# One core, a Fourier mixing block: a difference kept in PSUM, batch 0's inverse as one whole float32 product, and a self-paired channel by its sum less twice one part

## The chip, the cores and the metric

The kernel runs on one core of one Trainium2 chip. The metric is the time of one execution in device microseconds. Times are written in us, stretches of the run as us from the start of the profiled span. L905 is line 905 of the kernel before.

## The reference

The input x has 8 batches of 3136 tokens with 256 channels. Each batch is filtered along the tokens in the frequency domain, the result is mixed by a two-dimensional Fourier transform whose real part is added to it, and each token then goes through a normalisation and a two-layer perceptron with a residual:

```python
def _attn_ref(x, filt_r, filt_i):
    Y = np.fft.rfft(x, axis=1) * (filt_r + 1j * filt_i)[None]
    return np.fft.irfft(Y, n=x.shape[1], axis=1).astype(np.float32)

def _moe_ref(x, w_ch1, w_ch2):              # x is what _attn_ref gave
    mixed = np.real(np.fft.fft(np.fft.fft(x, axis=1), axis=2)).astype(np.float32)
    u = x + mixed
    un = (u - mean(u)) / sqrt(var(u) + 1e-6)
    return u + np.maximum(un @ w_ch1, 0.0) @ w_ch2      # 256 -> 1024 -> 256
```

The token transform of the filtered signal is the spectrum Y itself, so the kernel mixes straight from Y and needs the inverse transform only for the residual u.

## The kernel before

**Work and tiles.** Per batch: `first` and `spectrum` are the two stages of the forward transform (112 x 28 points), `spectrum` with the filter behind it. `inverse1` and `inverse2` are the two stages of the inverse (7 chunks `ch` or `c` each), with a turn through DRAM between them (`d2`, written from tile `bt`, read back as `b2`). `fold` makes sums and differences of channel pairs for the channel transform (`ef`, then `eo` as a float16 high and low part), `bring` scales the inverse and sends it to DRAM (`dy`). The tokens are then taken in 49 groups `g` of 256 pairs of rows: `fetch` loads the group's residual (`pages<-dy`, L1030), `prepare` adds the channel mixing (L1071 products, L1096 and L1121 additions) and makes the norm's statistics, `normalize` gives `ut`, and `products` runs eight steps per group: six products into `h` (L1318), `rectify` (ACT L1346, DVE L1348) and twelve products into `acc` (L1359), added to the residual in L1373. Batches 1 to 7 split each float32 operand into a float16 high and low part and run three float16 passes; batch 0 is worked in float32 where the time before the first step is concerned.

**Order.** Everything is placed by `Plan`, a planner in the program: each task yields its next engine with an estimated duration, takes buffers from rings of fixed size (`take`, `give`), and the planner writes down one fixed order per engine. On the chip each engine runs its list strictly in that order. The four PSUM banks of ring `psf` serve `first`, `spectrum` (from batch 1), both inverse stages and the mixing; the products have banks of their own (`psh`, `pso`). Ring `x16` holds three 2 KB scratch buffers, ring `ast` three buffers for DRAM writes. Almost all DMAs are issued from SP's one queue.

**The places that are touched.** In `inverse1` PE gives two banks per chunk, `ps[0]` and `ps[1]`, each from 64 x 64 corners of the array (L873, with L863 for the first chunk). From batch 1, ACT copies `ps[1]` to SBUF (L891), DVE makes sum and difference into SBUF (L895), ACT casts both to float16 (L901) and the low parts are the float32 value less the cast, both read from SBUF:

```python
            for i in range(2):
                pool_ = i >= LOW_ON_DVE[b > 1]
                yield ("POOL", 1.16) if pool_ else ("DVE", 0.65)
                (nc.gpsimd if pool_ else nc.vector).tensor_tensor(
                    bt[:, :, 1, i], sums[i], bt[:, :, 0, i], op=ALU.subtract
                )
```

(L905: batch 1 both on DVE, later batches one on DVE and one on POOL.) For batch 0 `inverse1` copies the two banks out as they are (L914) and sum and difference are made after the turn, in `inverse2`, by two DVE instructions per chunk on SBUF (L953). The float32 table `i1f` of batch 0 is later turned in place into the float16 table `i1` by `split_back` (ACT L679 and L681, POOL L683). `fold` sets row 0 of the difference, the channel pair that is its own mirror, by one more subtraction on one partition (L822 on DVE for batch 0, L825 on POOL after).

Of the kernel before, what the change touches and what calls it, by code (L numbers as in the profile page):

```python
# [37 lines left out]
TWIN = 0.83  # L38
BACKED = 6.5
LOW_ON_DVE = (2, 1)  # L40
# [168 lines left out]
def constants():  # L209
# [30 lines left out]
    even[0] = p % 2 == 0  # L240
# [44 lines left out]
    def both_halves(a):  # L285
# [5 lines left out]
    i1f = both_halves(i1.reshape(112, 29, 64).astype(np.float32))  # L291
# [11 lines left out]
        "c_i1f": np.ascontiguousarray(i1f),  # L303
        "c_i2f": both_halves(i2f),
# [11 lines left out]
def _program(ctx, tc, nc, a, NB):  # L316
# [46 lines left out]
    i1 = cp.tile([120, 29, 2, 64], F16, name="i1")  # L363
# [11 lines left out]
    i1f = i1.rearrange("p j l u -> p (j l u)").bitcast(F32).rearrange("p (j u) -> p j u", u=64)  # L375
# [10 lines left out]
    def z_page(ch):  # L386
        return pages[:, (ch + YBUFS) % (YBUFS + 2)].rearrange("p (l j c) -> p l j c", l=1, c=256)
# [41 lines left out]
    y16s = [cp.tile([128, 2, 8, 64], F16, name=f"y16_{h}") for h in range(4)]  # L429
    for t in y16s:  # L430
        nc.gpsimd.memset(t[:, :, :, 56:], 0.0)
# [131 lines left out]
    def first(b, q, t):  # L563
# [39 lines left out]
        home = (*("ast",) * 3, "un", "un", "u16", "u16", *("h",) * 4)[q % 11] if b == 0 else "ast"  # L603
        k = yield take(home)
        pool, bufs = (fp, 3) if home == "ast" else (mp, 4 if home == "h" else 2)
# [44 lines left out]
    def load_tables():  # L650
# [6 lines left out]
        for ch in range(7):  # L657
            yield "SP" if ch == 0 else "calm", 0.5, -78
            j = slice(4 * ch + (ch > 0), 4 * ch + 5)
            nc.sync.dma_start(i1f[:, j], a["c_i1f"][:, j])  # L660
# [11 lines left out]
    def split_back():  # L672
        yield until(("backs",))
        for ch in range(7):
            j = slice(4 * ch + (ch > 0), 4 * ch + 5)
            k = yield take("x16")
            whole = fp.tile([120, 4 + (ch == 0), 64], F32, tag="x16", name=f"i1f_{ch}", bufs=3)
# [6 lines left out]
            give("x16", k)  # L684
            done("i1", ch)

    def by_part(b, yt):
# [3 lines left out]
        v = yt.rearrange("p h (j s q) -> p h j s q", j=4, s=2)[..., :56]  # L691
        return v.rearrange("p h j s (r q) -> p h r j s q", r=2)

    def spectrum(b, ch, hf, t):
# [4 lines left out]
        if hf == 0:  # L699
# [3 lines left out]
            n = 448 if b else 512  # L703
            yts[b, ch] = k, pool.tile([128, 2, n], F32, tag=home, name=f"yt_{b}_{ch}", bufs=2), home
            if b == 0:
                yield "POOL", 0.2
                nc.gpsimd.memset(yts[b, ch][1].rearrange("p h (j q) -> p (h j) q", q=64)[:, :, 56:], 0.0)
# [56 lines left out]
        if b == 0:  # L764
            kp = yield take("psh")
            pt = spare(f"yT_{ch}_{hf}").rearrange("p (j c) -> p j c", j=4)
            yield "PE", 0.7
            for j in range(4):
                nc.tensor.transpose(pt[:, j], yt[:, hf, 128 * j : 128 * j + 128], ident)
# [3 lines left out]
            nc.scalar.copy(zs[b, ch][:, 0, :, 128 * hf : 128 * hf + 128], pt)  # L773
            give("psh", kp)
            done("z", b, ch, hf)
            return
        k = yield take(f"y16_{hf}")
# [18 lines left out]
    def fold(b, ch, t):  # L796
# [12 lines left out]
        if ch == 0:  # L809
# [4 lines left out]
            nc.vector.tensor_copy(es[:1, 1:2], ef[:1, 1, 0, 0:1])  # L814
# [783 lines left out]
```

## Time and profile before

| | |
|---|---|
| runs | 1465.88, 1466.61, 1467.34; median 1466.61 |
| profiled execution | 1467.97, its span 1466.2 |
| first step's product starts | 124.68 |
| busy share of the span | PE 92%, DVE 74%, ACT 58%, POOL 49% |
| mean granted TensorE clock | 0.963 |

The span is the time from the first to the last instruction of the profiled execution, which itself took 1.4 us more than the median run. PE's busy time counts pipelined matmuls, so two engines' shares are not alike. The granted clock is 1 at 2.4 GHz and 0.5 at 1.2 GHz.

### The profile page before, as it was taken

Reading aid. Unit: us, or ns where it says so; the run is one execution under the profiler, and the core shown is the slowest. Engines: PE = TensorE matmul, PEld = TensorE weight load, DVE = VectorE, ACT = ScalarE, POOL = GpSimd, SP = SyncE. Lnnn points to the kernel's source line nnn. Section 1 sums busy time; section 2 is a strip of 40 time slices with the busy share of each in tenths; the row PEclk is TensorE's granted clock in tenths of the full one; section 3 lists DMA queues with packets and bytes.
Section 4 is the critical chain, followed back from the end, with each engine's and each line's share of the span. In section 5 each row is a group of like instructions: output and inputs, shape, how many; then the busy total and the mean of one; then the engine's idle time right before and its main releaser. Section 6 shows DMA issues by size and latency. Waiting matters only on the chain.

```text
span 1466.2 us, 33150 instructions
## 1 busy us (share of the span) xinstructions
PE 1356.0 (92%) x12693; PEld 906.8 (62%) x12693; DVE 1082.1 (74%) x2199; ACT 850.3 (58%) x1605; POOL 719.9 (49%) x893
## 2 busy tenths in 40 slices
PE   4647998869999999999999999999999998999998
PEld 1423565547666666666666766667666665666666
DVE  5797688776778698787878787778858788564543
ACT  4367456754567557764577567755566664444341
POOL 2631197126861488325961776338833398132220
PEclk8757999989999999999999999999999999999999
DMA  8966788759696889769887989669794997643330
GB/s 279 261 187 191 193 161 202 195 174 227 138 230 191 192 192 200 189 176 241 172 221 217 203 199 230 178 166 218 170 252 128 226 193 158 158 114 107 93 85 29
DMA packets 359933, 268.89 MB, mean 183 GB/s; under 512 B 217751, under 2 KB 295007, under 8 KB 359775
## 3 DMA queue, kind: packets, MB, share of 16 engines
q1 hardware_dynamic: 359775, 266.79, 74.5%
q8 instruction: 99, 1.62, 0.5%
q14 instruction: 59, 0.48, 0.1%
HBM read 113.10 MB, written 102.76 MB: 147 GB/s over the span
## 4 chain that ended last, share of the span: by engine, by line
PE 61%; DVE 13%; POOL 7%; DMA 6%; issue 6%; ACT 5%; SPq 1%; DVEq 0%; POOLq 0%; ACTq 0%
PE h L1318 25%; PE acc L1359 24%; PE s L601 3%; PE y L968 2%; DMA x<-x 2%; DMA d<-ast 2%; DVE bt L905 2%; PE mix L1071 2%; PE i L873 2%; DVE h L1348 1%; DVE pages L1096 1%; DMA at<-d 1%; DVE t L743 1%; POOL y L784 1%; DVE st L1236 1%
## 5 line engine op out<-in xcount | busy, mean ns | idle before, releaser
L1359 PE MATMUL acc<-w2s,h 128*128 128x256 f16 x4704 | 589.7, 273 | 11.9 <-DVE pages L1373 11.9
L1318 PE MATMUL h<-ut,w1s 128*128 128x512 f16 x2352 | 580.4, 383 | 14.6 <-DVE h L1348 8.8
L1359 PEld LDWEIGHTS <-h 128*128 128x128 f16 x4704 | 453.1, 98 | 146.2 <-issue 25.7
L1348 DVE SCALAR_TENSOR_TENSOR h<-h,h 128x512 f16<-128x512 f32 x392 | 268.2, 685 | 250.4 <-ACT h L1346 249.2
L1346 ACT ACTIVATE h<-h 128x512 f16<-128x512 f32 x392 | 232.8, 594 | 295.0 <-PE h L1318 286.4
L1318 PEld LDWEIGHTS <-w1s 128*128 128x128 f16 x2352 | 225.8, 98 | 228.2 <-issue 28.4
L1293 POOL TENSOR_TENSOR u<-un,u 128x512 f16<-128x512 f32 x94 | 110.6, 1177 | 274.1 <-ACT u L1287 258.5
L1267 ACT ACTIVATE un<-pages,sb 128x256 f32<-128x256 f32 x196 | 109.6, 593 | 27.2 <-DVE sb L1217 24.4
L1121 POOL TENSOR_TENSOR pages<-sm,pages 128x508 f32<-128x508 f32 x48 | 61.8, 1289 | 122.7 <-ACT sm L1159 100.1
L837 POOL TENSOR_TENSOR eo<-ef,eo 128x448 f16<-128x448 f32 (+6 forms) x62 | 61.5, 996 | 100.6 <-ACT eo L834 70.7
L784 POOL TENSOR_TENSOR y<-yt,y 128x448 f16<-128x448 f32 x98 | 104.4, 1070 | 12.3 <-ACT y L782 12.0
L757 POOL TENSOR_TENSOR yt<-yt,t 128x224 f32<-128x224 f32 x98 | 67.5, 688 | 78.4 <-DVE t L743 77.9
L743 DVE SCALAR_TENSOR_TENSOR t<-s,pF,ft 128x448 f32<-128x448 f32 x126 | 83.7, 671 | 8.9 <-PE s L725 8.9
L1096 DVE SCALAR_TENSOR_TENSOR pages<-mix,alpha,pages 128x254 f32<-128x254 f32 (+2 forms) x188 | 83.5, 476 | 4.9 <-ACT sm L1159 3.5
L1236 DVE BATCH_NORM_STATS2 st<-pages 128x6 f32<-128x256 f32 x196 | 80.3, 410 | 8.9 <-POOL pages L1127 7.2
L993 ACT ACTIVATE ys<-y,alpha 128x512 f32<-128x512 f32 x110 | 70.9, 685 | 25.5 <-PE y L968 25.1
L782 ACT CAST y<-yt 128x448 f16<-128x448 f32 x98 | 54.9, 563 | 49.3 <-POOL yt L759 47.6
L905 DVE TENSOR_TENSOR bt<-sd,bt 128x512 f16<-128x512 f32 x56 | 79.5, 1428 | 0.6 <-ACT bt L901 0.6
L743 DVE SCALAR_TENSOR_TENSOR yt<-s,pF,ft 128x448 f32<-128x448 f32 x98 | 65.9, 673 | 15.6 <-PE s L725 14.8
L601 PE MATMUL s<-x,s 112*112 112x512 f16 x252 | 67.5, 390 | 9.5 <-DVE x L578 5.8
L895 DVE TENSOR_TENSOR sd<-i,sd 128x512 f32<-128x512 f32 x98 | 66.9, 682 | 12.0 <-ACT sd L891 10.2
L905 POOL TENSOR_TENSOR bt<-sd,bt 128x512 f16<-128x512 f32 x42 | 50.3, 1197 | 51.1 <-ACT bt L901 43.2
(171 smaller groups left out, 1800.0 us busy)
## 6 DMA issues: line engine op xcount, KB each, us to landing
x<-x SPq DMA_DIRECT2D x56, 448.0 KB
d<-ast SPq DMA_DIRECT2D x112, 224.0 KB
at<-d SPq DMA_DIRECT2D x56, 448.0 KB
d<-bt SPq DMA_DIRECT2D x112, 224.0 KB
pages<-d SPq DMA_DIRECT2D x112, 224.0 KB
out<-pages SPq DMA_DIRECT2D x98, 256.0 KB
pages<-dy SPq DMA_DIRECT2D x92, 256.0 KB
dy<-ys SPq DMA_DIRECT2D x96, 224.0 KB
```

What stands on the lines that cost most here:

```text
L601: nc.tensor.matmul(p, s1[:, hs], x16[:, hx], start=i == 0, stop=i == 2)
L743: nc.vector.scalar_tensor_tensor(out, p, pF[:, 1:2], f, op0=ALU.mult, op1=ALU.mult)
L784: nc.gpsimd.tensor_tensor(y16v[:, 1], yh, y16v[:, 0], op=ALU.subtract)
L905: (nc.gpsimd if pool_ else nc.vector).tensor_tensor(bt[:, :, 1, i], sums[i], bt[:, :, 0, i], op=ALU.subtract)
L1096: nc.vector.scalar_tensor_tensor(out, p, al, y, op0=ALU.mult, op1=ALU.add)
L1236: nc.vector.bn_stats(st[:, 2 * t + k], y[:, t, k])
L1267: nc.scalar.activation(un[:, k], y[:, t, k], AF.Identity, bias=sb[:, i, 1:2], scale=sb[:, i, 3:4])
L1293: nc.gpsimd.tensor_tensor(u16[:, :, :, 1], unv, u16[:, :, :, 0], op=ALU.subtract)
L1318: nc.tensor.matmul(p.rearrange("p (t k q) -> p t k q", t=2, k=2), w1s[:, d, hw, 128 * f : 128 * f + 128], utv[:, :, :, d, hx], start=i == ...
L1346: nc.scalar.activation(h[:, 0], p, AF.Relu)
L1348: nc.vector.scalar_tensor_tensor(h[:, 1], p, 0.0, h[:, 0], op0=ALU.max, op1=ALU.subtract)
L1359: nc.tensor.matmul(acc[:, kind], h[:, hh, c0 : c0 + 128], w2s[:, f, hw], start=f == 0 and kind == 0 and i == 0, stop=f == 7 and kind == 1 ...
```

## The change

Three things are done, and the buffers are laid out anew for them.

1. `inverse1` from batch 1: the difference is written back into PSUM, over `ps[1]`, and its cast and its low part are read from there. The sum goes into the scratch buffer `total` (batch 1: into PSUM, over `ps[0]`). In later batches cast and low part of the sum are a task of their own, `low_half`, on ACT and POOL. One scratch buffer is taken in place of two; the banks are held for longer.
2. Batch 0: `inverse1_whole` makes sum and difference in the product itself, with a table of 112 x 112 per slot in float32 (four products of 256 columns per chunk, two per bank, on the whole array), and `inverse2` reads them without an addition. Each half chunk is stored by two DMAs of 1 KB rows. Transposes and DRAM rows of batch 0 lose their padding and its memsets. The larger `i1f` shares its memory (`late`) with `i1` and with the `y16` buffers, so `i1` comes by DMA and `y16` is cleared after batch 0's last inverse product (`load_back`).
3. `fold`: row 0 of the difference becomes minus twice the second part (one ACT instruction on one partition), and the mixing table's row 0 is all ones, so that sum and minus twice one part make what was the difference.

The last three DRAM writes of batch 0's `first` go through `x16` buffers instead of waiting for `ast`, and the planner's start for batch 0's `inverse1` is moved from 6.5 to 3.8 steps.

```diff
-TWIN = 0.83
+TWIN = 0.86
+PASSES = ((0, 0), (1, 0), (0, 1))
-LOW_ON_DVE = (2, 1)
...
-    i1 = cp.tile([120, 29, 2, 64], F16, name="i1")
+    late = cp.tile([128, 2048 + 1856], F32, name="late")
+    i1f = late[:112, :3136].rearrange("p (j u) -> p j u", u=112)
+    i1 = late[:120, 2048:].bitcast(F16).rearrange("p (j l u) -> p j l u", l=2, u=64)
...
-        home = (*("ast",) * 3, "un", "un", "u16", "u16", *("h",) * 4)[q % 11] if b == 0 else "ast"
+        home = (*("ast",) * 3, "un", "un", "u16", "u16", *("h",) * 4, *("x16",) * 3)[q] if b == 0 else "ast"
...
-    def split_back():
-        yield until(("backs",))
-        for ch in range(7):
-            yield "ACT", 0.35
-            nc.scalar.copy(whole, i1f[:, j])
-            yield "ACT", 0.35
-            nc.scalar.copy(i1[:, j, 0], whole)
-            yield "POOL", 0.6
-            nc.gpsimd.tensor_tensor(i1[:, j, 1], whole, i1[:, j, 0], op=ALU.subtract)
+    def load_back():
+        yield until(("backs",))
+        yield "POOL", 0.7
+        nc.gpsimd.memset(y16a.rearrange("p i l j q -> p (i l j) q")[:, :, 56:], 0.0)
+        done("y16")
+        for i in range(2):
+            yield "calm", 1.7
+            j = slice(0, 13) if i == 0 else slice(13, 29)
+            nc.sync.dma_start(i1[:, j], a["c_i1"][:, j])
...
 def fold(b, ch, t):
-        if b == 0:
-            yield "DVE", 0.52
-            nc.vector.tensor_tensor(eft[:1, 1], yt[:1, 0, 0], yt[:1, 1, 0], op=ALU.subtract)
-        else:
-            yield "POOL", 0.64
-            nc.gpsimd.tensor_tensor(eft[:1, 1], yt[:1, 0, 0], yt[:1, 1, 0], op=ALU.subtract)
+        yield "ACT", 0.4
+        nc.scalar.activation(eft[:1, 1], yt[:1, 1, 0], AF.Copy, scale=-2.0)
...
+    def inverse1_whole(ch, h, t):
+        yield until(("z", 0, ch, 0), ("z", 0, ch, 1), ("i1f", ch))
+        kp = yield take("psf")
+        j = 4 * ch + 2 * h
+        p = bank(f"i1_0_{ch}_{h}")[:112].rearrange("p (j c) -> p j c", j=2)
+        yield "PE", 1.0
+        for i in range(2):
+            nc.tensor.matmul(p[:, i], i1f[:, j + i], zs[0, ch][:, 2 * h + i], start=True, stop=True)
+        k = yield take("ast")
+        yield "ACT", 0.58
+        nc.scalar.copy(bt, p)
+        give("psf", kp)
+        for i in range(2):
+            yield "SP", 0.33
+            nc.sync.dma_start(d2s[0][:, j : j + 2, i], bt[56 * i : 56 * i + 56])
...
 def inverse1(b, ch, t):                          # from batch 1
-            kx = yield take("x16", 2)
-            nc.scalar.copy(sums[1], ps[1])
-            give("psf", kp + 1)
-            for i, op in enumerate((ALU.add, ALU.subtract)):
-                yield "DVE", 0.7
-                nc.vector.tensor_tensor(sums[i], ps[0], sums[1], op=op)
-            give("psf", kp)
+        kx = yield take("x16")
+        nc.scalar.copy(total, ps[1])
+        late_sum = ps[0] if b == 1 else total
+        for out, op in ((ps[1], ALU.subtract), (late_sum, ALU.add)):
+            yield "DVE", 0.7
+            nc.vector.tensor_tensor(out, ps[0], total, op=op)
+        give(*(("x16", kx) if b == 1 else ("psf", kp)))
+        yield "ACT", 0.55
+        nc.scalar.copy(bt[:, :, 0, 1], ps[1])
+        if b > 1:
+            plan.spawn(low_half(b, ch, kx, total, bt), t)
+        yield "DVE", 0.66
+        nc.vector.tensor_tensor(bt[:, :, 1, 1], ps[1], bt[:, :, 0, 1], op=ALU.subtract)
+        give("psf", kp + 1)
+        if b == 1:
+            yield "ACT", 0.55
+            nc.scalar.copy(bt[:, :, 0, 0], ps[0])
+            yield "DVE", 0.66
+            nc.vector.tensor_tensor(bt[:, :, 1, 0], ps[0], bt[:, :, 0, 0], op=ALU.subtract)
+            give("psf", kp)
...
+    def low_half(b, ch, kx, total, bt):
+        yield "ACT", 0.6
+        nc.scalar.copy(bt[:, :, 0, 0], total)
+        yield "POOL", 1.18
+        nc.gpsimd.tensor_tensor(bt[:, :, 1, 0], total, bt[:, :, 0, 0], op=ALU.subtract)
...
 def inverse2(b):
-            if b == 0:
-                part, turned = bt[:, :, 0, 0], bt[:, :, 0, 1]
-                for out, op in ((ys[:120, 0:2], ALU.add), (turned, ALU.subtract)):
-                    yield "DVE", 0.65, t
-                    nc.vector.tensor_tensor(out, part, turned, op=op)
```

## Rows read from the trace of the kernel before

**Rows 1.** The page: the span, PE's and the other engines' busy time over the whole span, and the granted TensorE clock in tenths in 40 equal slices of 36.7 us.

```profile
span 1466.2 us, 33150 instructions
PE 1356.0 (92%) x12693; PEld 906.8 (62%) x12693; DVE 1082.1 (74%) x2199; ACT 850.3 (58%) x1605; POOL 719.9 (49%) x893
...
PEclk8757999989999999999999999999999999999999
```

**Rows 2.** Busy time of each engine by stretch. Columns: the stretch, its length, then busy us (and instructions) of PE, weight loads, DVE, ACT, POOL, then the mean granted clock, the DMA engines' share and GB/s.

```profile
41.00:124.60 83.60, 44.56 (x491) 28.52 (x489) 76.73 (x158) 48.12 (x102) 39.59 (x51) 0.66 0.84 235
124.60:1466.00 1341.40, 1292.64 (x12162) 870.47 (x12161) 983.85 (x2000) 785.38 (x1471) 671.76 (x820) 0.99 0.74 177
...
200.00:270.00 70.00, 64.07 (x645) 43.26 (x643) 63.12 (x107) 45.65 (x86) 48.73 (x59) 0.98 0.76 181
270.00:330.00 60.00, 43.30 (x349) 26.57 (x350) 42.81 (x96) 37.94 (x70) 13.37 (x15) 0.87 0.65 180
```

**Rows 3.** Who PE waited for from 125 us on: us in total, times, the longest.

```profile
PE acc L1359 <- DVE pages L1373: 11.9, 12, 3.1
PE h L1318 <- DVE h L1348: 8.8, 8, 2.6
```

**Rows 4.** Instructions in order of time on DVE, POOL and PE around 411 us: start, duration, engine, line, operation, tiles, shapes, count, and in brackets the engine's idle time before it and who ended it.

```profile
411.23 6.59 DVE L905 TENSOR_TENSOR bt<-sd,bt 128x512 f16<-128x512 f32 x1 [0.28 <-ACT bt L901]
...
411.28 1.03 POOL L837 TENSOR_TENSOR eo<-ef,eo 128x448 f16<-128x448 f32 x1
...
416.12 1.14 POOL L1293 TENSOR_TENSOR u<-un,u 128x512 f16<-128x512 f32 x1
...
418.53 0.71 PE L1359 MATMUL acc<-w2s,h 128*128 128x256 f16 x5 [3.09 <-DVE pages L1373]
```

**Rows 5.** The same view at three other places, DVE and then PE for each.

```profile
1208.04 6.47 DVE L905 TENSOR_TENSOR bt<-sd,bt 128x512 f16<-128x512 f32 x1
1215.75 1.46 PE L1318 MATMUL h<-ut,w1s 128*128 128x512 f16 x3 [2.56 <-DVE h L1348]
...
1239.07 5.52 DVE L905 TENSOR_TENSOR bt<-sd,bt 128x512 f16<-128x512 f32 x1
1245.89 1.73 PE L1318 MATMUL h<-ut,w1s 128*128 128x512 f16 x4 [2.34 <-DVE h L1348]
...
239.14 4.77 DVE L905 TENSOR_TENSOR bt<-sd,bt 128x512 f16<-128x512 f32 x2
245.76 0.59 PE L1318 MATMUL h<-ut,w1s 128*128 128x512 f16 x2 [1.50 <-DVE h L1348]
```

**Rows 6.** Three DVE lines over the whole span: count, then the shortest, median and longest duration in ns, and the starts of the first and last.

```profile
L905 DVE TENSOR_TENSOR bt<-sd,bt x56: 671/1084/6586, 208.7 to 1257.6; 128x512 f16<-128x512 f32 x56
L895 DVE TENSOR_TENSOR sd<-i,sd x98: 656/682/692, 203.1 to 1254.4; 128x512 f32<-128x512 f32 x98
L1213 DVE SCALAR_TENSOR_TENSOR sb<-mv,sb x50: 154/168/3697, 113.2 to 1410.8; 128x4 f32<-128x4 f32 x48, 128x2 f32<-128x2 f32 x2
```

**Rows 7.** Three stretches with a low granted clock (columns as in Rows 2), and PE's row before the first of them.

```profile
225.50:228.90 3.40, 3.40 (x25) 1.72 (x23) 2.27 (x4) 1.70 (x5) 2.67 (x4) 0.50 0.87 244
1215.30:1218.70 3.40, 2.95 (x8) 1.19 (x9) 3.40 (x6) 0.67 (x2) 2.33 (x4) 0.51 0.88 191
1246.10:1249.50 3.40, 3.40 (x12) 1.67 (x11) 3.19 (x10) 0.94 (x2) 0.00 (x0) 0.50 0.29 92
...
224.20 1.04 PE L1359 MATMUL acc<-w2s,h 128*128 128x256 f16 x8 [2.29 <-DVE pages L1373]
```

**Rows 8.** In order of time, batch 1's first chunk behind `inverse1`'s products: ACT's copy, DVE's sum and difference, DVE's two low parts.

```profile
195.11 0.59 ACT L891 COPY sd<-i 128x512 f32<-128x512 f32 x1 [1.07 <-PE i L873]
203.14 1.40 DVE L895 TENSOR_TENSOR sd<-i,sd 128x512 f32<-128x512 f32 x2
208.72 2.60 DVE L905 TENSOR_TENSOR bt<-sd,bt 128x512 f16<-128x512 f32 x2
```

**Rows 9.** First DVE's groups between 41 and 125 us that the change removes (count, busy us, mean ns, idle before), then two lines of POOL and ACT over the whole span with durations as in Rows 6.

```profile
L822 DVE TENSOR_TENSOR ef<-yt 1x224 f32<-1x224 f32 x7 | 4.0, 572 | 0.0
L953 DVE TENSOR_TENSOR ys<-pages 120x512 f32<-120x512 f32 x3 | 2.3, 780 | 0.7 <-DMA dy<-ys 0.7
L953 DVE TENSOR_TENSOR pages<-pages 120x512 f32<-120x512 f32 x3 | 2.1, 692 | 0.1
...
L825 POOL TENSOR_TENSOR ef<-yt x49: 647/651/1102, 187.4 to 1265.6; 1x224 f32<-1x224 f32 x49
...
L1232 ACT COPY pages<-keep x8: 401/404/405, 110.9 to 1290.4; 1x256 f32<-1x256 f32 x8
```

**Rows 10.** In order of time: SP's last stores of batch 0's first inverse stage and the loads behind them, the first L953 on DVE, and on PE the last whole chunk of that stage (16 instructions, two for each of eight float32 products) and the second stage's first product. The last row is from the chain that ended last: 14 instructions of float32 products of 512 columns at full clock, two for each product.

```profile
83.66 0.77 SPq L919 DMA_DIRECT2D d<-bt  x2
87.55 11.00 SPq L937 DMA_DIRECT2D pages<-d  x6
...
94.35 0.68 DVE L953 TENSOR_TENSOR ys<-pages 120x512 f32<-120x512 f32 x1
...
80.39 1.09 PE L873 MATMUL i<-pages,i 56*64 56x256 f32 x16 [0.68 <-ACT pages L773]
95.12 1.08 PE L968 MATMUL y<-ys,i2f 56*64 56x256 f32 x2 [0.34 <-issue]
...
147.63 6.12 PE s L590 x14
```

More of the change, by code (lines that the diff above doesn't have):

```diff
@@ L428, in _program @@
     pF = cp.tile([128, 2], F32, name="pF")
-    y16s = [cp.tile([128, 2, 8, 64], F16, name=f"y16_{h}") for h in range(4)]
-    for t in y16s:
-        nc.gpsimd.memset(t[:, :, :, 56:], 0.0)
+    y16a = late[:, :2048].bitcast(F16).rearrange("p (i l j q) -> p i l j q", i=4, l=2, q=64)
+    y16s = [y16a[:, h] for h in range(4)]
     sxs, alphas, esps = {}, {}, {}
@@ L670, in load_tables @@
         done("i2f")
-    def split_back():
+    def load_back():
         yield until(("backs",))
-        for ch in range(7):
-            j = slice(4 * ch + (ch > 0), 4 * ch + 5)
-            k = yield take("x16")
-            whole = fp.tile([120, 4 + (ch == 0), 64], F32, tag="x16", name=f"i1f_{ch}", bufs=3)
-            yield "ACT", 0.35
-            nc.scalar.copy(whole, i1f[:, j])
-            yield "ACT", 0.35
-            nc.scalar.copy(i1[:, j, 0], whole)
-            yield "POOL", 0.6
-            nc.gpsimd.tensor_tensor(i1[:, j, 1], whole, i1[:, j, 0], op=ALU.subtract)
-            give("x16", k)
-            done("i1", ch)
+        yield "POOL", 0.7
[5 more added lines that the diff above has]
+            nc.sync.dma_start(i1[:, j], a["c_i1"][:, j])
+            for ch in range(3 * i, 3 + 4 * i):
+                done("i1", ch)
     def by_part(b, yt):
@@ L776, in spectrum @@
             return
+        yield until(("y16",))
         k = yield take(f"y16_{hf}")
@@ L874, in inverse1 @@
                             ps[s][64 * c : 64 * c + 64, jj],
-                            table[row, e],
+                            i1[row, e, lw],
                             z[row, lx, 2 * c + jj],
                             start=i == 0 and jj == (ch == c == 0),
-                            stop=i == len(passes) - 1 and jj == 1,
+                            stop=i == len(PASSES) - 1 and jj == 1,
                         )
-        backs[b, ch] = True
-        if b == 0 and len(backs) == 7:
-            done("backs")
@@ new lines, in inverse1 @@
+        give("big", 21 * b + 7 + ch)
+        kx = yield take("x16")
+        total = fp.tile([128, 2, 256], F32, tag="x16", name=f"sd_{b}_{ch}", bufs=3)
+        yield "ACT", 0.58
+        nc.scalar.copy(total, ps[1])
[4 more added lines that the diff above has]
+        give(*(("x16", kx) if b == 1 else ("psf", kp)))
+        k = yield take("ast")
@@ new lines, in inverse1 @@
+        bt = fp.tile([128, 2, 2, 2, 256], F16, tag="ast", name=f"bt_{b}_{ch}", bufs=3)
+        yield "ACT", 0.55
[11 more added lines that the diff above has]
+            give("psf", kp)
+        else:
+            yield until(("low", b, ch))
@@ L921, in inverse1 @@
         done("d2", b, ch)
+    def low_half(b, ch, kx, total, bt):
[3 more added lines that the diff above has]
+        nc.gpsimd.tensor_tensor(bt[:, :, 1, 0], total, bt[:, :, 0, 0], op=ALU.subtract)
+        give("x16", kx)
+        done("low", b, ch)
     backs = {}
     def load_b2(b):
-        yield until(*(("d2", b, ch) for ch in range(7)))
+        yield until(*((("d2", b, ch) if b else ("d2", 0, ch, h)) for ch in range(7) for h in range(1 if b else 2)))
         if b:
@@ L966, in inverse2 @@
                                 e, half, turn = h if js == 0 else 2 + 2 * h, js, h
-                            moving = bt[row, half, lx, turn] if b or turn else ys[row, half]
                             nc.tensor.matmul(
@@ L970, in inverse2 @@
                                 table[row, e],
-                                moving,
+                                bt[row, half, lx, turn],
                                 start=i == 0 and js == 0,
@@ L1531, in _program @@
                 plan.spawn(spectrum(b, ch, h, t), t)
-            t = s0 + half * (2 * ch + 1) + BACKED
-            plan.spawn(inverse1(b, ch, t), t)
             t = s0 + half * (2 * ch + 1) + 2.2
             plan.spawn(fold(b, ch, t), t)
+            t = s0 + half * (2 * ch + 1) + (BACKED if b else 3.8)
+            if b:
+                plan.spawn(inverse1(b, ch, t), t)
+                continue
+            for h in range(2):
+                plan.spawn(inverse1_whole(ch, h, t + h), t + h)
         plan.spawn(load_b2(b), brought(b, 0))
```

95 lines of the change are left out of this document (38 added, 57 removed).

## The prediction, made before the changed kernel ran

> **What bounds the kernel now.** I read the page first: PE is busy for 92% of the span and the granted clock is low mostly at the start [rows 1]. So I cut the span where the products begin. From 124.6 us on PE is busy for 1292.6 of 1341.4 us [rows 2]: that stretch is bound by PE's own work, none of which the change removes, and all that can be won there is the 48.8 us in which PE is idle, and the time lost to the lower clock behind such pauses. Before 124.6 it is the other way round: PE is busy for 44.6 of 83.6 us and DVE for 76.7 [rows 2]. The start is bound by DVE's list, with the transfers of batch 0 beside it.
>
> Then I asked whom PE waits for in the long stretch. The two largest entries are both DVE: L1373, which empties the banks of the second product, and L1348, which makes the low part of `h`: 20.7 us together [rows 3]. Neither is slow itself; what counts is what stood in front of it on DVE. In the list of instructions around 411 us that is one L905 of 6.59 us, while POOL runs instruction behind instruction, the last of them from 416.12 to 417.26; DVE's ends 0.56 us later, and PE has then stood for 3.09 us [rows 4]. The same picture stands at 1208, at 1239 and at 239 us, with PE idle for 2.56, 2.34 and 1.50 us [rows 5]. L905 takes 671 ns at best, 1084 in the median and 6586 at worst; L895, as large, but with one of its inputs in PSUM, never over 692 in 98 times [rows 6]. I read this as DVE losing SBUF reads to POOL when both its inputs lie in SBUF, for as long as POOL has work without a gap.
>
> The Trainium skill, "SBUF — State Buffer", section "Who interferes with whom", says that a DVE instruction with two SBUF inputs and a GpSimd (here POOL) instruction that reads SBUF exclude each other, and that the loser waits until the first one finishes. By that wording L905 could lose to one POOL instruction at a time, 1.0 to 1.2 us here, and the four stalls would shrink by some 4.6 us instead of 9.5; the rows show a wait over a whole run of them.
>
> **The change part by part.** The sum is made against the profiled execution, 1467.97 us; the median run is 1.4 lower.
>
> *L905.* From batch 1 the low part on DVE reads PSUM and one SBUF tile, the operands of L895. Its price is L895's 682 ns [rows 6]; the difference written back to PSUM is an operation that the trace doesn't show, between L895's 656 at best and L905's median of 1084, and I take 682, as PSUM is already one of L895's sides. At the upper end 56 such writes cost 22 us of DVE, which is no bound there (983.9 of 1341.4 [rows 2]). What matters is the four stalls: 3.09 + 2.56 + 2.34 + 1.50 = 9.5 us, which I take off whole (below: nothing, if another instruction takes L905's place in the same queue).
>
> *What hangs on the stalls.* The granted clock fell to the lower level for 3.4 us each at 225.5, 1215.3 and 1246.1, just behind stalls of 2.29, 2.56 and 2.34 us [rows 5, 7]. Work at 1.2 GHz for 3.4 us loses 1.7, three times 5.1. I take two of three: 3.4 (0 to 5.1). The stall of 2.29 us itself ends on L1373 at 224.20 [rows 7], in a stretch where DVE is busy for 63.1 of 70 us [rows 2]. There batch 1's two low parts take 2.60 us per chunk [rows 8] and would take 1.36, 8.7 us less over seven chunks; I take the 2.3 off too.
>
> *The start.* DVE loses seven L822 (4.0 us) and six of the fourteen L953 (2.3 + 2.1): 8.4 us before the first step [rows 9]. That is the upper end. The data's path is the other limit. Batch 0's last chunk is stored at 83.66, its loads are issued at 87.55, and L953 starts at 94.35, behind DVE's other work, with PE's product at 95.12 waiting for it [rows 10]. The two loads of the first chunk are 0.46 MB, at the 235 GB/s of this stretch [rows 2] 1.9 us; so some 4.9 us of that wait are DVE's and go away, and 4.0 more come from the L822 ahead. Against it: the whole products. A float32 instruction of 512 columns takes 6.12/14 = 0.437 us, so one of 256 columns 0.219, two for each of four products 1.75 us per chunk, against 1.09 for the eight corner products now [rows 10]. Only the last chunk's 0.7 is on the path; the other six lie in PE's idle time, and uncovered all seven would cost 4.6. Two more stores for the last chunk at 0.385 each [rows 10]: 0.8. The table grows from 0.89 to 1.40 MB: 2.2 us of transfer at that rate, on the path or not; the first part of `i1`, 0.40 MB, is issued behind the last product and may stand ahead of the loads: 1.7 us. So 1.5 to 5.4 against 8.9, leaving 3.5 to 7.4: I take 5.5, and 2 to 8.4 for the range. Next late, once L953 is gone, is the store and reload of `dy`, which no edit touches. L679, L681, L683 and the padding's memsets go at nothing: before the first step ACT is busy for 48.1 and POOL for 39.6 of 83.6 us [rows 2], and no product there waits for them; without that cover they would add at most what they take themselves.
>
> The Trainium skill, "TensorEngine Tiling (Array Packing)", section "Theoretical Speedup", gives matrices of at most 64 in both dimensions up to 4x from tiles. The change gives these tiles up; by the rule the whole product is twice as dear, 2.2 us per chunk, where the row's rate says 1.75. It would put 0.4 more on the path.
>
> *Row 0 of the difference.* POOL loses 49 times 0.65 = 32 us; ACT gains 56 instructions of about 0.40, the price of L1232, together 22 us [rows 9]. ACT is busy for 58% [rows 1], and what waits behind is the cast of `eo`, which no longer waits for POOL. If that cover fails, each stands in front of an L1346: 49 times 0.40, 20 us; I put 1 on.
>
> *What comes back.* Other instructions with two SBUF inputs stay on DVE. L1213 took 3697 ns once, against a median of 168 [rows 6]. When POOL has a long run, one of those may now stand there: one stall in four, 2.5 back.
>
> Sum: 5.5 + 9.5 + 3.4 + 2.3 - 1 - 2.5 = 17.2 off 1467.97, so 1450.8 for the profiled execution and 1449.4, say 1449, for the median.
>
> **The rivals.**
>
> *A: the stall changes its instruction.* The next DVE instruction with two SBUF inputs takes L905's place, or it was not POOL's reads that held it. For it: L1213's 3697. Against it: L1213 is one instruction of 4 columns per group. Then about the start and 3 us of the rest are left: 1458.
>
> *B, on the other side: PSUM banks in batch 1.* Batch 1 now keeps both banks until its last low part. In its first chunk the copy begins at 195.11, the sum is done at 204.54, the last low part at 211.32 [rows 8]: one bank was held for 9.4 us and the other for 0.6, and both would be for 16.2. Seven chunks lie in some 70 us, so a chunk has 10 us of four banks, 40 bank-us; inverse alone goes from 10 to 32, and the spectra, the mixing and the second stage draw on the same ring. The extra 22 over four banks is 5.6 us per chunk; half of that, as DVE's own delay shrinks, makes batch 1 some 20 us late. Nothing would cover it: from 270 to 330 us PE already idles for 16.7 [rows 2] on batch 1's results. 1449 + 20 and the 4 of gains around 225 and 245 that go: 1473. It decides from 2.5 us per chunk on. Against it: most of the hold is DVE's lateness (7.4 us from the copy's end to the sum's start), a queue that gets shorter.
>
> *C: nothing to measure.* The start's path takes the upper prices (5.4, products uncovered) and the stalls return elsewhere: 1466, within the 0.2% (2.9 us) about which a measurement of this kernel can't tell.
>
> *D: more.* Batch 1 comes early enough to fill 10 of the 16.7 idle us between 270 and 330, where nothing was taken: 1439.
>
> **How the numbers follow.** Forecast 0.46 (1443 to 1455), D 0.16, A 0.21, C 0.06, B 0.11. Faster is forecast, D and A: 0.83; same 0.06; slower 0.11. The range leaves out B and the upper half of C, and some of D's lower side: 1433 to 1465.
>
> **What would show it.** No DVE low part of `inverse1` over 0.75 us; the low parts on POOL unchanged; no DVE instruction of several us in front of an idle PE; PE's idle time from the first step on near 33 instead of 48.8, and fewer stretches at the lower clock; the first step 5 to 6 us earlier; L953's place taken by nothing on DVE. I am wrong if a long DVE instruction still stands in front of L1373 or L1348 (A), if PE's idle time between 200 and 330 us grows while PE or ACT wait for banks of `psf` (B), or if the first step starts no earlier than 123.

## The result and the profile after

The changed kernel takes 1424.18 us (median of four runs, 1423.1 to 1426.21), the kernel before 1466.97 beside it: a ratio of 0.9709, interval 0.9692 to 0.9725. That is 42.8 us less, where the sum forecast 17.2; 1424 lies below the range (1433 to 1465). The direction was right, the size wrong.

The page of the profiled execution after: the span, busy times, and the granted clock in 40 slices, to be read against [rows 1].

```profile
span 1422.7 us, 32916 instructions
...
PE 1347.1 (95%) x12637; PEld 910.9 (64%) x12637; DVE 1024.7 (72%) x2178; ACT 865.0 (61%) x1647; POOL 666.5 (47%) x827
...
PEclk8767999989999999999999999999999999999999
```

Busy time by stretch of the changed kernel, with the columns of [rows 2]; the last two rows are for comparison with experiments below.

```profile
41.00:119.10 78.10, 51.20 (x489) 37.73 (x490) 65.65 (x145) 48.44 (x99) 31.65 (x41) 0.70 0.97 270
119.10:1422.70 1303.60, 1276.32 (x12115) 865.53 (x12114) 937.27 (x1991) 799.49 (x1515) 627.23 (x771) 0.99 0.77 183
200.00:270.00 70.00, 68.29 (x694) 46.12 (x696) 59.92 (x123) 53.93 (x104) 36.40 (x47) 1.00 0.87 213
270.00:330.00 60.00, 48.51 (x489) 32.82 (x482) 45.06 (x104) 32.56 (x63) 29.01 (x38) 0.91 0.88 221
...
345.00:1200.00 855.00, 846.11 (x8414) 577.34 (x8412) 657.68 (x1379) 565.20 (x1078) 471.06 (x576) 1.00 0.85 199
...
900.00:1100.00 200.00, 198.22 (x1893) 134.51 (x1891) 153.84 (x323) 132.94 (x252) 95.89 (x116) 1.00 0.80 194
```

From the first step on PE is idle for 1303.60 - 1276.32 = 27.3 us, where [rows 2] gave 48.8. The difference is 21.5 us, half of the gain. The first step's product starts at 119.1. Before, its first instruction started at 124.0 (the 124.68 in the table of the kernel before is where the chain that ended last takes that product up), so 4.9 us come from the start. After, and then before:

```profile
L1328 PE MATMUL h<-ut,w1s x12: 379/564/631, 119.1 to 123.5; 128*128 128x512 f16 x12
...
123.96 5.58 PE L1318 MATMUL h<-ut,w1s 128*128 128x512 f16 x12 [0.82 <-ACT ut L1277]
```

From the first step on the granted clock is low in two stretches after the change:

```profile
119.10:123.10 4.00, 3.51 (x10) 1.17 (x10) 3.85 (x12) 1.95 (x3) 2.38 (x4) 0.57 1.05 275
300.10:310.30 10.20, 4.96 (x43) 3.07 (x44) 8.58 (x27) 4.35 (x10) 7.46 (x10) 0.50 1.06 225
```

In the kernel before there are seven in which PE works (from 124.0, 225.5, 273.0, 321.0, 1123.0, 1215.3 and 1246.1 us; three stand in [rows 7]), and this is the row that sums them:

```profile
sum 37.10, PE 28.91 PEld 12.97 DVE 28.90 ACT 19.07 POOL 12.79; mean PE 4.13 PEld 1.85 DVE 4.13 ACT 2.72 POOL 1.83
```

PE worked for 28.9 us at about half speed, and works for 3.51 + 4.96 = 8.5 now: 20.4 less, worth about 10.2. Idle time, start and clock make 21.5 + 4.9 + 10.2 = 36.6 of the span's 43.5 us. Some 5 of the rest are work that PE now does ahead of the first step: 32 more of batch 0's float32 products into `y`, which cost 3.0 us behind it before, and 16 more mixing products, 1.8 us. What was left of the former behind the first step, before (two rows) and after:

```profile
L968 PE MATMUL y<-ys,i2f 56*64 56x256 f32 x32 | 2.8, 426 | 0.0
L968 PE MATMUL y<-pages,i2f 56*64 56x256 f32 x32 | 2.4, 376 | 0.0
...
L978 PE MATMUL y<-pages,i2f 56*64 56x256 f32 x32 | 2.2, 389 | 0.0
```

The last 2 us are not accounted for. PE's busy time ahead of the first step (51.20 us, before 44.56 [rows 2]) is no measure of the moved work, as the whole products alone are 3.6 us dearer there.

Whom PE waits for from 119 us on, after, to be read against [rows 3]:

```profile
PE s L721 <- DMA at<-d: 11.5, 2, 9.7
PE s L607 <- DVE x L584: 2.0, 5, 0.7
PE h L1328 <- ACT ut L1287: 1.7, 1, 1.7
...
PE h L1328 <- DVE h L1358: 0.8, 1, 0.8
PE acc L1369 <- DVE pages L1383: 0.7, 2, 0.4
```

The two entries of DVE fell from 20.7 to 1.5 us. Waits for DMA rose from 5.9 to 12.5; these are the two entries before:

```profile
PE h L1318 <- DMA ut<-u: 4.8, 2, 4.4
...
PE s L724 <- DMA at<-d: 1.1, 1, 1.1
```

One long pause is left, 9.66 us of PE ahead of 305.34, for batch 2's loads of `at`, the turn behind `first`; in time order, PE and then SP's queue:

```profile
294.72 0.95 PE L1081 MATMUL mix<-mix,eo 128*128 128x129 f16 x16
305.34 0.23 PE L721 MATMUL s<-s,at 112*128 112x56 f16 x1 [9.66 <-DMA at<-d]
...
297.99 0.32 SPq L625 DMA_DIRECT2D d<-ast  x1
299.37 1.25 SPq L1306 DMA_TRANSPOSE ut<-u  x1
300.72 0.52 SPq L653 DMA_DIRECT2D at<-d  x1
```

The low part on DVE and the difference and sum, to be read against [rows 6]:

```profile
L914 DVE TENSOR_TENSOR bt<-i,bt x49: 658/681/693, 198.8 to 1210.1; 128x512 f16<-128x512 f32 x49
...
L905 DVE TENSOR_TENSOR i<-i,sd x56: 672/692/700, 194.4 to 1207.8; 128x512 f32<-128x512 f32 x56
L905 DVE TENSOR_TENSOR sd<-i,sd x42: 660/692/693, 337.5 to 1208.6; 128x512 f32<-128x512 f32 x42
```

With one operand in PSUM the low part never takes longer than 693 ns, and the write back into PSUM costs 692, where 682 was taken.

### The profile page after: what moved, and what is told of

It is laid out like the page before. It is cut to its first block, busy times and chain, and to the rows that moved or that the text cites. A ratio compares the mean times of both kernels' runs of the same rounds, so it can differ in the third digit from the quotient of the medians.

```text
span 1422.7 us, 32916 instructions
## 1 busy us (share of the span) xinstructions
PE 1347.1 (95%) x12637; PEld 910.9 (64%) x12637; DVE 1024.7 (72%) x2178; ACT 865.0 (61%) x1647; POOL 666.5 (47%) x827
## 4 chain that ended last, share of the span: by engine, by line
PE 47%; DVE 4%; ACT 2%; DMA 2%; POOL 1%; issue 1%; SPq 1%; POOLq 0%; ACTq 0%; DVEq 0%
PE acc L1369 20%; PE h L1328 19%; PE s L607 2%; PE y L978 2%; PE mix L1081 1%; PE i L890 1%; DMA x<-x 1%; DVE pages L1106 1%; PE s L721 1%; PE s L722 1%; DVE h L1358 1%; DVE st L1246 1%; DMA at<-d 0%; ACT h L1356 0%; DVE x L584 0%
## 5 line engine op out<-in xcount | busy, mean ns | idle before, releaser
L1277 ACT ACTIVATE un<-pages,sb 128x256 f32<-128x256 f32 x196 | 110.9, 596 | 16.7 <-DVE sb L1227 16.6
L782 POOL TENSOR_TENSOR late<-yt,late 128x448 f16<-128x448 f32 x98 | 102.8, 1054 | 17.4 <-ACT late L780 16.5
L740 DVE SCALAR_TENSOR_TENSOR t<-s,pF,ft 128x448 f32<-128x448 f32 x126 | 84.0, 675 | 10.2 <-PE s L722 9.7
L1383 DVE SCALAR_TENSOR_TENSOR pages<-acc,beta,pages 128x512 f32<-128x512 f32 x98 | 70.4, 743 | 15.7 <-PE acc L1369 15.6
L721 PE MATMUL s<-s,at 112*128 112x56 f16 x896 | 61.5, 190 | 19.9 <-DMA at<-d 17.6
L780 ACT CAST late<-yt 128x448 f16<-128x448 f32 x98 | 55.1, 563 | 33.5 <-POOL yt L756 26.2
L584 DVE SCALAR_TENSOR_TENSOR x<-x,sx,x 112x512 f16<-112x512 f32 x84 | 70.1, 857 | 4.3 <-ACT x L582 4.2
```

The source lines that it names most:

```text
L721: nc.tensor.matmul(o, w, s2[:, U, 0].rearrange("p (r k) -> p r k", r=2), start=True, stop=False)
L740: nc.vector.scalar_tensor_tensor(out, p, pF[:, 1:2], f, op0=ALU.mult, op1=ALU.mult)
L782: nc.gpsimd.tensor_tensor(y16v[:, 1], yh, y16v[:, 0], op=ALU.subtract)
L1277: nc.scalar.activation(un[:, k], y[:, t, k], AF.Identity, bias=sb[:, i, 1:2], scale=sb[:, i, 3:4])
```

## The experiments

The median of the kernel before moved between 1467 and 1474 us from one set of runs to the next, so kernels are compared by their ratio to it; "us less" is that ratio's share of 1467. TWIN is the planner's estimate for an inverse product. Changing it alters no instruction and no byte, only the order that is written down: apart from waits on semaphores, every line has the same count of instructions in the five traces of the old work, and in the two of the new.

| work | TWIN: ratio to before (95%), us less |
|---|---|
| as before | 0.83: 1, 0; 0.86: 0.9966 (0.9944 to 0.9987), 5; 0.88: 0.9993 (0.9962 to 1.0025), 1; 0.78: 0.9870 (0.9837 to 0.9902), 19; 0.815: 0.9781 (0.9748 to 0.9815), 32 |
| part 1 | 0.83: 0.9914 (0.9884 to 0.9945), 13; 0.84: 0.9837 (0.9805 to 0.9868), 24 |
| part 3 | 0.83: 0.9961 (0.9937 to 0.9985), 6; 0.80: 0.9805 (0.9769 to 0.9841), 29 |
| parts 1, 3 | 0.83: 0.9825 (0.9793 to 0.9856), 26 |
| part 2 | 0.86: 0.9895 (0.9853 to 0.9937), 15; 0.87: 0.9734 (0.9706 to 0.9763), 39 |
| parts 1, 2 | 0.86: 0.9789 (0.9753 to 0.9825), 31; 0.87: 0.9706 (0.9677 to 0.9734), 43 |
| parts 2, 3 | 0.86: 0.9898 (0.9868 to 0.9929), 15; 0.81: 0.9714 (0.9684 to 0.9745), 42 |
| all three | 0.86: 0.9709 (0.9692 to 0.9725), 43; 0.84: 0.9834 (0.9815 to 0.9853), 24; 0.86 with batch 1 a step earlier: 0.9688 (0.9662 to 0.9714), 46 |

Part 2 stands for batch 0's whole product with all that hangs on it (tables, the `x16` homes in `first`, the 3.8 steps).

**First, one part or one cause at a time.** Parts 1 and 3 put alone on the kernel before, and TWIN alone:

```text
b_psum: part 1 of the change on the kernel before (difference in PSUM, low_half)
b_fold: part 3 on the kernel before (row 0 by ACT, mixing row of ones)
b_twin:
-TWIN = 0.83
+TWIN = 0.86
```

> The kernel before with part 1 alone: from batch 1 the difference goes back to PSUM and its cast and low part read it there; batch 0 and the fold stay as they were. Theory L (DVE instructions with two SBUF inputs lose to POOL's runs, the stalls of PE and the falls of the clock behind them hang on those): most of what the long stretch gained (38.6 us of the span) is here, 1430 to 1445 us; no DVE low part of inverse1 over 0.75 us and PE idle from the first step on under 32 us. Theory F (POOL's 32 us less work in the fold is what ends the stalls): 1455 to 1462. Theory R (the planner's new order is what helps, whatever part is changed): a time that follows neither, and DVE instructions that are no shorter in front of the PE stalls that remain.

Measured 1455.77: 10 us above theory L's range, and at the lower end of theory F's. As theory L asked, no low part is over 0.75 us, and of PE's waits the two DVE entries fell from 20.7 to 1.5 us. But waits for DMA rose from 5.9 to 16.0, and PE is idle for 39.7 us from the first step on, where theory L asked for under 32. The largest wait for DMA and the two DVE entries:

```profile
PE h L1331 <- DMA ut<-u: 13.6, 5, 4.9
...
PE acc L1372 <- DVE pages L1386: 0.9, 2, 0.7
...
PE h L1331 <- DVE h L1361: 0.6, 1, 0.6
```

> The kernel before with part 3 alone: row 0 of the difference as minus twice one part on ACT, the mixing table's row 0 all ones. Theory L: POOL's queue is 32 us shorter but the 56 DVE low parts with two SBUF inputs stay, so long ones stay: 1458 to 1468 us. Theory F: 1440 to 1452, POOL's runs shorter and no L905 over 3 us.

Measured 1462.76, in theory L's range.

> The kernel before with the planner's figure TWIN at 0.86 in place of 0.83 and nothing else: the same instructions, placed in a slightly different order. Theories L and F: within 6 us of the kernel before, 1460 to 1472. Theory R: it moves by 8 us or more.

Measured 1463.62, in the range of theories L and F. From these alone I read that the two SBUF inputs, the order and POOL's list were each worth little. For the order this reading was wrong, as the last runs show.

The sharpest of the four gives DVE's low parts back two SBUF inputs in the changed kernel, the minuend being a fixed part of the filter table. In the two traces the instructions stand in the same order on every engine, so here the order is held:

```diff
-            nc.vector.tensor_tensor(bt[:, :, 1, 1], ps[1], bt[:, :, 0, 1], op=ALU.subtract)
+            nc.vector.tensor_tensor(bt[:, :, 1, 1], held, bt[:, :, 0, 1], op=ALU.subtract)
...
+        held = ft[:, 0, 0, :512].rearrange("p (j c) -> p j c", j=2)
```

> The changed kernel with one operand of 56 DVE instructions changed: the low part of the difference (and in batch 1 of the sum) subtracts the cast from a fixed part of the filter table in SBUF in place of PSUM, so that both inputs lie in SBUF again; planner's durations, order and all else are the same, the low parts themselves are not the right values. Theory L: these instructions get long again (median near 1.1 us, some of 3 to 6), PE's idle time from the first step on goes up by 15 to 25 us and the clock falls more often: 1440 to 1455 us. Theories F and R: under 1430, as the order and POOL's work are those of the changed kernel.

Measured 1433.32, a ratio of 0.9766 (0.9736 to 0.9796): 8 us more than the changed kernel, 2 to 15 by the intervals' ends. That lies between the ranges, below theory L's and above the others'. The low part is long again, by line and then in time order on DVE and POOL:

```profile
L915 DVE TENSOR_TENSOR bt<-ft,bt x49: 659/1022/4803, 201.7 to 1217.6; 128x512 f16<-128x512 f32 x49
...
993.11 4.80 DVE L915 TENSOR_TENSOR bt<-ft,bt 128x512 f16<-128x512 f32 x1
...
992.83 1.27 POOL L806 TENSOR_TENSOR ef<-yt 128x224 f32<-128x224 f32 x2
994.06 1.05 POOL L782 TENSOR_TENSOR late<-yt,late 128x448 f16<-128x448 f32 x1
995.07 1.16 POOL L936 TENSOR_TENSOR bt<-sd,bt 128x512 f16<-128x512 f32 x1
996.18 1.18 POOL L831 TENSOR_TENSOR eo<-ef,eo 128x256 f16<-128x256 f32 x2
```

The operand alone brings the long instruction back, while POOL runs without a gap; this part of the reading of [rows 4] is shown. A long low part need not idle PE, though: beside this one, the longest, PE worked on without a pause. The forecast priced what hangs on it at 9.5 + 2.3 + 3.4 - 2.5 = 12.7 us. Not all of the 8 need be the operand's: in the profiled executions the first step starts 3.1 us later (122.2 against 119.1), before any of the exchanged instructions has run. From the first step on PE is idle for 1308.00 - 1276.56 = 31.4 us, 4.2 more than in the changed kernel, where theory L expected 15 to 25 more:

```profile
122.20:1430.20 1308.00, 1276.56 (x12115) 865.00 (x12114) 958.31 (x1991) 799.12 (x1515) 638.53 (x771) 0.99 0.77 182
```

**Then the parts in pairs**, two put on the kernel before, or one or two undone on the changed kernel:

```text
b_both: parts 1 and 3 on the kernel before
a_nofold: the changed kernel, part 3 undone
a_nopsum: the changed kernel, part 1 undone
a_whole: the changed kernel, parts 1 and 3 undone
```

> The kernel before with parts 1 and 3, batch 0 as it was. Alone they gave 11.5 and 4.6 us, the whole change 42.8. Theory S (PE stalls when either DVE's or POOL's list is late; only when both get shorter do the stalls behind 345 us and the falls of the clock go): less than the sum of the two, 1435 to 1446 us, PE idle behind 345 us near 10 instead of 22. Theory N (the larger half of the gain comes with batch 0's new inverse, as batch 1 then runs earlier): the sum of the two, 1449 to 1455, PE idle behind 345 us 15 or more. Theory L as it was put on record (DVE's reads lost to POOL are most of it) has already failed in size.

> The changed kernel with parts 1 and 3 undone: batch 0's whole product, its buffers and the scratch buffers of its first stage alone. Theory S: the start 5 us earlier and some of the idle time up to 345 us, 1453 to 1460 us, PE idle behind 345 us near 20. Theory N: 1435 to 1448.

> The changed kernel with part 3 undone: row 0 of the difference by a subtraction on POOL again (batch 0: on DVE), the mixing table as before. Theory S: POOL's 32 us come back and the stalls with them, 1435 to 1448 us. Theory N: within 6 us of the changed kernel, 1424 to 1430.

> The changed kernel with part 1 undone: from batch 1 sum and difference in SBUF, two casts, low parts on DVE and POOL as before. Theory S: 1440 to 1452 us, DVE instructions of several us with two SBUF inputs again. Theory N: 1430 to 1438, of which the 9 us of the run with SBUF inputs are most.

Measured 1443.91, 1453.99, 1439.45 and 1454.33: the first three in theory S's ranges, the last 2 us above its range. The parts do not add: part 1 was worth 13 us alone and 28 on top of the others (0.9898 less 0.9709), part 3 nothing on top of part 2 and 12 on top of parts 1 and 2. I took this for two lists, DVE's and POOL's, that both have to get shorter (theory S). But the trace with part 1 undone has no low part on DVE over 1.65 us; it loses its time between 900 and 1100 us, where PE waits for batch loads:

```profile
900.00:1100.00 200.00, 182.61 (x1710) 123.17 (x1709) 142.68 (x302) 124.19 (x235) 93.47 (x112) 0.95 0.79 185
...
PE s L722 <- DMA at<-d: 8.4, 1, 8.4
PE h L1316 <- DMA ut<-u: 5.2, 1, 5.2
```

PE is idle for 17.4 us there, against 1.8 in the changed kernel, with POOL and DVE less busy than there. That looks like no list that is too long, but like a place where the written order lets PE reach the batch's products before their loads. So the next runs changed the order alone.

**The order alone, first round.**

```text
a_twin84 (the changed kernel):              TWIN = 0.86 -> 0.84
a_nopsum81 (part 1 undone):                 TWIN = 0.86 -> 0.81
b_psum84 (part 1 on the kernel before):     TWIN = 0.83 -> 0.84
a_b1 (the changed kernel): batch 1's first stage due at -8 in place of -7 steps
```

> The changed kernel with one number changed: the planner's estimate TWIN for an inverse product is 0.84 in place of 0.86. Every instruction and every byte is the same; only the order written down for the engines differs, and by the planner's own list it now holds pauses of PE near 900 to 1100 us. Theory O (a good part of the gain, and of what single parts seem to lose, is the order that the planner happens to write): pauses as in the kernel with part 1 undone, 8.4 and 5.2 us there, with 3.4 to 5 us of clock behind them, so 13 to 20 us slower than the changed kernel, 1437 to 1444. Theory S (shorter lists on DVE and POOL are the gain): within 5 us, as the same step did in the kernel before, 1419 to 1429.

Measured 1447.37, ratio 0.9834: 18 us more than the changed kernel with the same instructions, 3 us above theory O's range. Between 900 and 1100 us, and whom PE waits for there:

```profile
900.00:1100.00 200.00, 183.72 (x1749) 124.03 (x1748) 140.18 (x302) 125.09 (x239) 91.83 (x114) 0.95 0.80 190
...
PE s L721 <- DMA at<-d: 7.9, 1, 7.9
PE mix L1081 <- DVE sd L905: 4.9, 1, 4.9
```

> The changed kernel with part 1 undone, as before (1454.3 with TWIN 0.86), now with TWIN 0.81, at which the planner's list has no long pause of PE behind 345 us. The work is that of the earlier run. Theory O: the pauses of 8.4 and 5.2 us at 961 and 1032 us and the clock behind them go, 17 to 19 us: 1432 to 1442. Theory S: part 1's work costs what it cost there: 1449 to 1459.

Measured 1430.27, ratio 0.9714, 2 us below theory O's range: with a different number in the planner, part 1 undone costs nothing that can be measured, and the idle time of 17.4 us between 900 and 1100 has become 2.0:

```profile
900.00:1100.00 200.00, 197.99 (x1894) 134.96 (x1892) 151.99 (x328) 135.17 (x255) 100.73 (x120) 1.00 0.79 192
```

> The kernel before with part 1 alone, as in the earlier run (1455.8 with TWIN 0.83), now with TWIN 0.84, at which the planner's list has no long pause of PE behind 345 us. Theory O: the pauses of 2.2, 4.9 and 4.2 us at 964, 967 and 1284 us and the clock behind them go, 11 to 16 us: 1439 to 1446, so that part 1 alone is worth 21 to 28 us. Theory S: 1451 to 1461, part 1 alone worth 12 as measured.

Measured 1447.47, ratio 0.9837, 1 us above theory O's range: nearly twice what part 1 alone had seemed to be worth. Theory S falls: all three moved as theory O says, each 1 to 3 us outside its range.

> The changed kernel with batch 1's first stage due one step earlier (-8 in place of -7). The one long pause left is 9.7 us at 296, PE waiting for batch 2's loads, with 10.2 us at the lower clock behind it. If batch 2's chain comes late only because batch 1's did, some 5 to 10 us of pause and half the clock's 5 go: 1409 to 1419. If batch 2's chain is bound by its own transfers, nothing: 1421 to 1428.

Measured 1425.61, ratio 0.9688, the same as the changed kernel within the intervals. The 9.66 us ahead of 305 became 5.82 ahead of 297 and 3.88 ahead of 303; nothing was won, and the time lies in the range for a chain bound by its own transfers.

**The order alone, second round: is it all of the gain?**

```text
b_twin88, b_twin78, b_twin815 (the kernel before): TWIN = 0.83 -> 0.88, 0.78, 0.815
a_whole87 (part 2 alone):                          TWIN = 0.86 -> 0.87
a_nofold87 (part 3 undone):                        TWIN = 0.86 -> 0.87
b_fold80 (part 3 on the kernel before):            TWIN = 0.83 -> 0.80
```

> The kernel before with TWIN 0.88 in place of 0.83, at which the planner's list has no pause of PE behind 345 us and shorter ones from 200 to 345. Theory O (the order is most of the gain, whatever the work): the old work gets what the changed kernel got behind 120 us, 1435 to 1450. Theory K (the old work's loss is stalls behind long DVE instructions, which no order foresees; in the trace of before the 22.4 us of PE's idle time behind 345 us are mostly these): L905 still over 4 us several times, 1458 to 1469, as with 0.86 (1463.6).

Measured 1474.55, above both ranges. The kernel before took 1474 us beside it; by the ratio, 0.9993, it would be 1466 at 1467, in theory K's range. Its low part is still long, and PE's busy time from 345 to 1200 us is low:

```profile
L905 DVE TENSOR_TENSOR bt<-sd,bt x56: 679/836/6664, 206.7 to 1262.0; 128x512 f16<-128x512 f32 x56
...
345.00:1200.00 855.00, 826.22 (x8079) 561.20 (x8078) 655.88 (x1326) 532.61 (x1004) 483.39 (x590) 0.99 0.84 194
```

> Part 2 alone (parts 1 and 3 undone on the changed kernel), 1454.0 with TWIN 0.86, now with 0.87, at which the planner's list has pauses of some 13 us only from 200 us on. Theory O: falls to within 10 us of the changed kernel, 1424 to 1434. Theory K: the low parts keep both inputs in SBUF and POOL keeps its runs, so long DVE instructions stay (in the earlier run nine from 2.0 to 5.4 us); at most the pause of 10.1 us at 305 and its 5 of clock go: 1440 to 1454.

Measured 1434.48, ratio 0.9734, at the upper end of theory O's range: 24 us less than with 0.86, though the low part keeps both inputs in SBUF.

> Part 3 undone on the changed kernel, 1439.5 with TWIN 0.86, now with 0.87, at which the planner's list has no long pause behind 345 us. Theory O, and theory K too (part 1 has taken the low parts out of POOL's way): 1423 to 1433. Theory S (POOL's 49 instructions cost what they cost, whatever the order): 1436 to 1443.

Measured 1429.59, ratio 0.9706, in the range of theories O and K: part 3 undone costs nothing, either.

> The kernel before with TWIN 0.78 in place of 0.83: by the planner's list the tightest of the old work's orders, with no pause of PE behind 345 us. Theory O (the gain is order, and the old work too has a good one): 1430 to 1450. Theory K (the old work meets long DVE instructions in whatever order, several over 4 us; idle time behind 345 us 22 us or more): 1456 to 1475.

Measured 1451.46, ratio 0.9870, between the two ranges: 19 us less than the kernel before, with a low part of 6.0 us still in it.

> The kernel before with TWIN 0.815: a fifth order of the old work, with one short pause behind 345 us in the planner's list. Theory O: 1430 to 1450. Theory K: 1456 to 1475.

Measured 1438.77, ratio 0.9781: 32 us less than the kernel before, with every instruction of it. This decides for theory O. A low part of 5.4 us still stands in it, but PE waits for the first of the two DVE entries for 2.0 us and for the second not at all. The low part by line, PE's wait, and PE from 345 to 1200 us with TWIN 0.815:

```profile
L905 DVE TENSOR_TENSOR bt<-sd,bt x56: 657/980/5449, 211.3 to 1231.4; 128x512 f16<-128x512 f32 x56
...
PE acc L1359 <- DVE pages L1373: 2.0, 3, 0.9
...
345.00:1200.00 855.00, 846.44 (x8371) 578.01 (x8369) 667.17 (x1375) 551.47 (x1037) 510.27 (x620) 1.00 0.86 200
```

And the same stretch of the kernel before:

```profile
345.00:1200.00 855.00, 838.51 (x8308) 570.47 (x8306) 667.45 (x1356) 542.76 (x1022) 495.06 (x606) 1.00 0.83 197
```

From 345 to 1200 us PE is idle for 16.5 us in the kernel before, for 28.8 with TWIN 0.88, for 8.6 with 0.815 and for 8.9 in the changed kernel. The old work in a better order is as well fed there as the new.

> Part 3 alone (1462.8 with TWIN 0.83, where pauses of 7.1 and 9.2 us stood at 310 and 323 us and the clock was low for 23.9 us behind them), now with TWIN 0.80, at which the planner's list has about half of these pauses. Theory K (part 3 shortens POOL's list, and with it the runs behind which DVE stands; the rest was order): 8 us of pause and 7 of clock go, 1443 to 1452. If POOL's 49 instructions matter for nothing: 1456 to 1468.

Measured 1441.8, ratio 0.9805: 1 us below theory K's range, but no better than the old work with TWIN 0.815, so it says nothing for part 3.

## Why the prediction was too small

**What bounds the kernel: right.** The gain is idle time (21.5 us), the clock (10.2), the start (4.9) and work of PE that came to lie ahead of the first step (some 5), which the sum had not.

**The start: near, and in part luck.** 5.5 was forecast, 4.9 measured. But the start hangs on the order too: with TWIN alone the old work's first step starts between 122.1 and 126.2 us (five orders), the new work's at 118.0 or 119.1, so the difference could have been anything from 3 to 8; with part 3 undone and TWIN 0.87 it starts at 125.1. The whole product was priced a little low. At a granted clock of 1 the last chunk's eight instructions took 1.98 us, against 1.09 for the old ones [rows 10]: 0.9 more, where the sum had 0.7 and the rule cited beside it gives 1.1.

```profile
77.08 1.98 PE L852 MATMUL i<-pages,late 112*112 112x256 f32 x8
```

**The low part in PSUM: the mechanism is right, its size with the order held 8 us (2 to 15), the start's 3.1 included, against 12.7.** Price and write-back came out at 681 and 692 ns against 682. No DVE low part is over 0.75 us, as the prediction asked. Over all runs the operand bounds the stalls: in the eight kernels whose low part reads PSUM, PE waits for the two DVE entries for 1.5 to 5.0 us in all, in the twelve with two SBUF inputs for 2.0 to 20.7. How large they are with two SBUF inputs is a matter of the order. With part 1 undone and TWIN 0.81, a low part takes up to 4.40 us, PE waits for the two entries for 5.0, and nothing measurable is lost. What I listed as four stalls of the kernel were four stalls of one order.

**Row 0, B and the rest.** ACT's 56 instructions cost nothing visible (part 3 undone at TWIN 0.87 has the same ratio), so the 1 us was harmless. Rival B is refuted where it was placed: from 200 to 270 us PE is busy for 68.29 us against 64.07 [rows 2]. Rival A's successor instruction does not appear in the changed kernel. Of D, 5.2 of 10 us came: PE idles for 11.5 us from 270 to 330, where it idled for 16.7.

**The step that failed** is the sum's frame: "The sum is made against the profiled execution". I took that execution's other pauses as the kernel's, and let the edits remove only stalls that stand in front of an edited line. But the front matter says that a planner writes the order anew from estimated durations, and every edit, TWIN most directly, gives it other estimates. Neither a term nor a rival stood for that. The runs show its size: the same old work between ratios of 1 and 0.978 in five orders, 32 us; the same new work between 0.971 and 0.983 in two, 18 us.

In the sum's terms, idle time was forecast at 9.5 + 2.3 - 2.5 - 1 = 8.3 and came to 21.5. The two DVE entries gave 19.2: the 11.8 of the sum, and 7.4 of other pauses on the same two lines that the sum left in place. The longest of these, with no DVE instruction over 1.5 us in the 9 us ahead of it, is

```profile
1122.87 2.46 PE L1359 MATMUL acc<-w2s,h 128*128 128x256 f16 x12 [2.18 <-DVE pages L1373]
```

Waits for DMA took 6.6 back, and all other waits fell by 8.9. The clock term was forecast at 3.4 and came to 10.2: 4.9 from the three stretches of the sum, 5.3 from others. That an order alone can do this, TWIN 0.815 shows on the old work: PE is idle for 29.7 us from its first step on, against 48.8.

**How much is work?** The best orders found without part 2 have ratios of 0.978 to 0.984, those with it 0.969 to 0.973: some 10 us, of which the start is about 5. Parts 1 and 3 add nothing measurable to part 2 once its order is good (0.9734 alone; 0.9706, 0.9714 and 0.9709 with either or both, up to 4 us). By these orders, of the 43 us some 10 to 14 would be the new work and some 30 the order, the kernel before being that far from a better order of its own. This is an estimate from the best of a few orders and no separation: except in the operand's run the order could not be held while the work changed. The reverse of that run, a PSUM operand put into the old order, was not tried. That the planner's estimates fit one kind of work better than another is open too.

## What to carry to other kernels

Where a program writes its own schedule from estimates, every edit rolls a new schedule: before forecasting, ask how far one estimate, moved by a few per cent, moves the same kernel, and put that spread into the range. Judge a part by several orders with and without it, not by one run each: part 1 read as 13, 28 or 0 us here, depending on the order. To price one mechanism, find the edit that leaves the schedule alone and changes only an operand. And when an edit removes a wait, look at which waits came in its place: part 1 alone took 19 us of waits for DVE away, and waits for DMA took 10 back.

## What was not expected of the hardware

A DVE instruction with two SBUF inputs waited for a run of POOL instructions and not for one: 4.80 us, while POOL's instructions, none over 1.2 us, followed each other without a gap; [rows 4] show the same over 6.59 us. The Trainium skill, "SBUF — State Buffer", section "Who interferes with whom", has the loser wait until the first one finishes; neither trace bears out a wait for a single instruction. The same instruction with a PSUM input was never over 693 ns beside the same POOL list.

The low clock is a second price of a pause, and not in proportion to it. With the pause of 9.66 us the granted clock was 0.50 for 10.2 us, from 300.1, while PE still stood, to 310.3. Near the ends of those of 2.3 to 2.6 us in [rows 5, 7] it was low for 3.4 us each, in which PE worked for 2.95 to 3.40. Behind the longer one of 3.09 us in [rows 4] it did not fall.
